# Retention layer and gated feed-forward on one core: the decay table by products instead of Exp rows, a moved table load, and one queue for the first loads

## The chip, the cores and the metric

The kernel runs on 1 core of a Trainium2 chip. The metric is device time in microseconds (us) of one execution. Each median below is over all runs. The kernel before was run again on the same chip beside every group of experiments, with medians of 248.31 to 248.34 us. A ratio is the mean time of one kernel's runs over that of the other's in the same rounds, so it is not quite the ratio of the medians that I quote.

PE is the matmul engine, ACT is ScalarE, DVE is VectorE, POOL is GpSimd, and SP is SyncE, which here only issues loads and stores. In this kernel PE's results stand in PSUM and all other tiles in SBUF; an eviction is the copy of a result from PSUM to SBUF. A load lands when its data are there.

"Span" is the length of the profiled execution in its trace; it is some 1.7 us shorter than that execution's time. "Granted clock" is the mean share of full speed that PE, the matmul engine, was given.

## The reference

Two stages. The first is a retention recurrence over q, k, v of shape (4 batches, 8 heads, 768 tokens, 64):

```python
gamma = 1.0 - 2.0 ** (-5.0 - np.arange(H, dtype=np.float32))
scale = 1.0 / np.sqrt(D)
for t in range(S):
    state = gamma[None, :, None, None] * state + np.einsum('bhd,bhe->bhde', k[:, :, t], v[:, :, t])
    y[:, :, t] = scale * np.einsum('bhd,bhde->bhe', q[:, :, t], state)
```

The second takes y, as 3072 tokens of 512, through a feed-forward layer with d_ff = 1536:

```python
gate = 1.0 / (1.0 + np.exp(-(x @ w_gate)))
val = x @ w_val
return (gate * val @ w_out).astype(np.float32)
```

## The kernel before

The recurrence is cut into chunks of 128 tokens, six to a batch. Decay is taken out of the recurrence: v is multiplied by a table `tabv` that grows with the token, and the sum is multiplied by a table `taby` that shrinks with it. `taby` holds scale x gamma^t for 768 tokens and all heads, two heads in the partitions of each of 4 blocks of columns. ScalarE (ACT) makes it, row by row:

```python
def make_taby(cols):
    for p in range(NP):          # NP = 4
        nc.scalar.activation(taby[:, p, cols], toky[:, cols], AX.Exp, scale=lgp[:, p:p + 1], bias=lsc)

def transposes(g):
    # ... 8 transposes of kn[g], qn[g] on PE into the one PSUM buffer tp
    nc.scalar.activation(qkT[g], tp, AX.Copy)          # the eviction

def scale_v(g, eng):                                   # both inputs in SBUF
    eng.tensor_tensor(vs[g], vf[g], tabv[:, g % NCH, :].unsqueeze(2).to_broadcast([C, H, D]), op=ALU.mult)

def y_out(g):                                          # y is in PSUM, taby in SBUF
    # ...
    nc.vector.tensor_tensor(xT[g // 4][:, :, col:col + C], y[g], taby[:, :, c * C:(c + 1) * C], op=ALU.mult)
```

The loads are issued in the order of use. Chunk 0 comes over the queues of SP and ScalarE as f32, everything else over GpSimd's (POOL) queue, which casts k, q and the weights to bf16 on the way (v stays f32):

```python
nc.sync.dma_start(out=kf, in_=src(k, 0))
nc.scalar.dma_start(out=qf, in_=src(q, 0))
load_v(0, nc.sync)
# ... iota for toky over 768 columns, load_chunk(1), load_chunk(2)
load_gate_val(0)
load_chunk(3)
for s in range(1, NFF // 2):
    load_gate_val(s)
load_chunk(4)
for s in range(4):
    load_out(s)
for g in range(5, 8):
    load_chunk(g)
```

The start of the kernel is scheduled by hand. `keep_on(n)` is n small products that are meant to keep PE's clock up while it waits:

```python
make_taby(slice(0, 256))
# ... casts of chunk 0
keep_on(36); transposes(0); keep_on(8); scale_v(0, nc.vector); scores(0); state(0); state_out(0); masks(0); keep_on(8)
make_taby(slice(256, 384))
transposes(1); scale_v(1, nc.vector); inter(0); intra(0); y_out(0)
keep_on(10); scores(1); state(1); state_out(1); masks(1); inter(1); keep_on(10)
make_taby(slice(384, 512))
transposes(2); intra(1); scale_v(2, nc.vector); y_out(1)
# ... chunk 2 likewise
make_taby(slice(512, 768))
nc.scalar.preload_act_table(AX.Sigmoid)
intra(2); y_out(2); scale_v(3, nc.vector); keep_on(8)
up(0, 0, 0, 384)                                       # the first up-projection
```

After that, attention of later chunks is woven into the feed-forward products, in a fixed order on PE.

Of the kernel before, what the change touches and what calls it, by code (L numbers as in the profile page):

```python
# [9 lines left out]
F32 = mybir.dt.float32  # L10
BF16 = mybir.dt.bfloat16
I32 = mybir.dt.int32
AX = mybir.ActivationFunctionType
ALU = mybir.AluOpType
# [3 lines left out]
def kernel(  # L18
# [10 lines left out]
    nc = tc.nc  # L29
    B, H, S, D = q.shape  # L30
# [4 lines left out]
    NP = H // 2  # L35
    KT = D_MODEL // 128
    NFF = D_FF // 128
    scale = 1.0 / math.sqrt(D)
    lg = [math.log(1.0 - 2.0 ** (-5.0 - h)) for h in range(H)]

    ctx.enter_context(tc.manual_schedule())
    const = ctx.enter_context(tc.tile_pool(name="const", bufs=1))
# [12 lines left out]
    def src(x, g):  # L55
        b, c = divmod(g, NCH)
        return x[b, :, c * C:(c + 1) * C, :].rearrange("h s d -> s h d")

    def load_v(g, eng):
        vf[g] = ld.tile([C, H, D], F32, tag="vf", name="vf", bufs=8)  # L60
        eng.dma_start(out=vf[g], in_=src(v, g))  # L61

    def load_kq(g):
        kn[g] = ld.tile([C, H, D], BF16, tag="kn", name="kn")
        qn[g] = ld.tile([C, H, D], BF16, tag="qn", name="qn")
        nc.gpsimd.dma_start(out=kn[g], in_=src(k, g))  # L66
        nc.gpsimd.dma_start(out=qn[g], in_=src(q, g))  # L67

    def load_chunk(g):
        load_kq(g)  # L70
        load_v(g, nc.gpsimd)
# [5 lines left out]
    def load_gate_val(s):  # L77
        cols = slice(s * 256, (s + 1) * 256)
        for dst, w in ((wg, moe_w_gate), (wv, moe_w_val)):
            nc.gpsimd.dma_start(out=dst[:, :, cols],  # L80
                                in_=w.rearrange("(kk p) n -> p kk n", p=128)[:, :, cols])
# [6 lines left out]
    kf = const.tile([C, H, D], F32, name="kf")  # L88
    qf = const.tile([C, H, D], F32, name="qf")
    nc.sync.dma_start(out=kf, in_=src(k, 0))  # L90
    nc.scalar.dma_start(out=qf, in_=src(q, 0))
    load_v(0, nc.sync)
    tokv = const.tile([128, NCH], I32, name="tokv")
    nc.gpsimd.iota(tokv, pattern=[[C, NCH]], base=0, channel_multiplier=1)
    ident = const.tile([128, 128], BF16, name="ident")
    make_identity(nc, ident)
    toky = const.tile([128, S], I32, name="toky")
    nc.gpsimd.iota(toky, pattern=[[1, S]], base=0, channel_multiplier=0)
    load_chunk(1)
    causal = const.tile([128, 128], F32, name="causal")  # L100
    nc.gpsimd.memset(causal, 1.0)
# [7 lines left out]
    lgp = const.tile([128, NP], F32, name="lgp")  # L109
    lsc = const.tile([128, 1], F32, name="lsc")  # L110
    nc.vector.memset(lsc, math.log(scale))
    for p in range(NP):
        nc.vector.memset(lgp[0:D, p:p + 1], lg[2 * p])
        nc.vector.memset(lgp[D:128, p:p + 1], lg[2 * p + 1])
    zbd = [const.tile([128, NP, C], BF16, name=f"zbd{i}") for i in range(2)]
    for t in zbd:
        nc.vector.memset(t, 0.0)
    taby = const.tile([128, NP, S], F32, name="taby")

    def make_taby(cols):  # L120
        for p in range(NP):
            nc.scalar.activation(taby[:, p, cols], toky[:, cols], AX.Exp, scale=lgp[:, p:p + 1], bias=lsc)  # L122

    causal4 = causal.unsqueeze(1).to_broadcast([128, NP, 128])

# [4 lines left out]
    def pair(t, p):  # L130
        return t[:, 2 * p:2 * p + 2, :].rearrange("s h d -> s (h d)")

    def transposes(g):
        tp = pa.tile([128, 2 * NP, C], BF16, tag="tp", name="tp")
        for i, x in enumerate((kn[g], qn[g])):
            for p in range(NP):
                nc.tensor.transpose(tp[:, i * NP + p, :], pair(x, p), ident)  # L137
        qkT[g] = at.tile([128, 2 * NP, C], BF16, tag="qkT", name="qkT", bufs=3)
        nc.scalar.activation(qkT[g], tp, AX.Copy)  # L139

    def scale_v(g, eng):
        vs[g] = ld.tile([C, H, D], BF16, tag="vs", name="vs", bufs=4)
        eng.tensor_tensor(vs[g], vf[g], tabv[:, g % NCH, :].unsqueeze(2).to_broadcast([C, H, D]),  # L143
                          op=ALU.mult)
# [16 lines left out]
    def inter(g):  # L161
        y[g] = pa.tile([128, NP, C], F32, tag="y", name="y")
        if g % NCH > 0:
            for p in range(NP):
                nc.tensor.matmul(y[g][:, p, :], zbd[(g - 1) % 2][:, p, :], qkT[g][:, NP + p, :],  # L165
                                 start=(p == 0), stop=False, skip_group_check=True)
# [18 lines left out]
    def intra(g):  # L185
        first = g % NCH == 0
        for p in range(NP):
            for i, st in enumerate((stA[g], stB[g])):
                nc.tensor.matmul(y[g][i * D:(i + 1) * D, p, :], vs[g][:, 2 * p + i, :], st[:, p, :],  # L189
                                 start=(first and p == 0), stop=True, skip_group_check=True)  # L190
# [60 lines left out]
    def keep_on(n):  # L251
        u = pf.tile([128, 512], F32, tag="ff", name="ff")
        for _ in range(n):
            nc.tensor.matmul(u[:, :128], ident, ident, start=True, stop=True)  # L254


    load_gate_val(0)
    load_chunk(3)
    for s in range(1, NFF // 2):
        load_gate_val(s)  # L260
    load_chunk(4)
    for s in range(4):
        load_out(s)
# [2 lines left out]

    kn[0] = ld.tile([C, H, D], BF16, tag="kn", name="kn")
    qn[0] = ld.tile([C, H, D], BF16, tag="qn", name="qn")
    make_taby(slice(0, 256))
    nc.vector.tensor_copy(kn[0], kf)  # L270
    nc.scalar.copy(qn[0], qf)
    keep_on(36)
# [5 lines left out]
    state_out(0)  # L278
    masks(0)
    keep_on(8)  # L280
    make_taby(slice(256, 384))
    transposes(1)
    scale_v(1, nc.vector)
    inter(0)
# [5 lines left out]
    state_out(1)  # L290
    masks(1)
    inter(1)
    keep_on(10)
    make_taby(slice(384, 512))
    transposes(2)
    intra(1)
    scale_v(2, nc.vector)
    y_out(1)
# [4 lines left out]
    masks(2)  # L303
    inter(2)
    keep_on(12)
    make_taby(slice(512, 768))
    nc.scalar.preload_act_table(AX.Sigmoid)  # L307
    intra(2)
    y_out(2)
    scale_v(3, nc.vector)  # L310
# [62 lines left out]
```

## Time and profile before

| kernel before | value |
|---|---|
| time | 248.33 us (three runs, 248.3 to 248.36) |
| span, granted clock of the profiled run | 246.4 us, 0.997 |
| first up-projection on PE | 18.98 us |
| q of chunk 5: landed, transposed | 43.68, 44.72 us |

The page's first part gives busy time of each engine, its share of the span, and the number of instructions:

```profile
PE 234.1 (95%) x1816; PEld 123.3 (50%) x1816; DVE 101.5 (41%) x168; ACT 106.0 (43%) x191; POOL 91.5 (37%) x111
```

PE is busy for 95% of the span, so it idles for some 12 us at most. Here is the timeline of VectorE (DVE) before, around the end of chunk 0. Its columns are start, length, engine, line, operation, output and inputs, shapes, and in brackets the idle time before it and what ended that:

```profile
9.63 0.69 DVE L143 TENSOR_TENSOR vs<-vf,tabv 128x512 bf16<-128x512 f32 x1 [0.30 <-DMA vf<-in_v_dram]
10.24 0.68 DVE L197 TENSOR_TENSOR xT<-y,taby 128x512 bf16<-128x512 f32 x1
```

Two multiplications of the same size, each some 0.7 us, one right behind the other.

### The profile page before, as it was taken

How to read it: one execution, taken by the hardware profiler on the slowest of the kernel's cores; microseconds unless marked ns; L12 is line 12 of the kernel's file. 1: busy time of each engine (PE TensorE's matmuls, PEld its weight loads, DVE VectorE, ACT ScalarE, POOL GpSimd, SP SyncE). 2: the span in 40 equal slices, each digit the busy share in tenths (PEclk: the TensorE clock that was granted, in tenths of full speed). 3: DMA queues.
4: the chain of work that ended last, by engine and by line, in shares of the span. 5: the costliest groups of instructions: out<-in, count | busy, mean ns of one | idle time of the engine just before them, and what ended most of it. 6: DMA issues, size and time to landing. Idle time of an engine off the chain costs nothing.

```text
span 246.4 us, 4449 instructions
## 1 busy us (share of the span) xinstructions
PE 234.1 (95%) x1816; PEld 123.3 (50%) x1816; DVE 101.5 (41%) x168; ACT 106.0 (43%) x191; POOL 91.5 (37%) x111
## 2 busy tenths in 40 slices
PE   7689998997999999999999999999999999999993
PEld 7565644554455554445554445544445554444441
DVE  2565444563446631246631256541256532234300
ACT  7788333425444431454443444342444542233221
POOL 8986574987999912961111001111000000000000
PEclk9999999999999999999999999999999999999998
DMA  9999999999999932994012100002100002200022
GB/s 146 181 198 196 192 213 203 176 208 232 229 174 127 188 80 84 145 180 61 3 41 78 54 3 3 0 17 92 64 0 3 0 0 88 85 0 3 0 85 85
DMA packets 64212, 24.13 MB, mean 98 GB/s; under 512 B 51969, under 2 KB 59649, under 8 KB 64193
## 3 DMA queue, kind: packets, MB, share of 16 engines
q0 software_dynamic: 57616, 16.78, 62.2%
q1 hardware_dynamic: 5536, 6.82, 8.2%
q10 hardware_dynamic: 1040, 0.26, 0.5%
q8 instruction: 14, 0.23, 0.4%
q14 instruction: 6, 0.04, 0.1%
HBM read 28.31 MB, written 6.29 MB: 140 GB/s over the span
## 4 chain that ended last, share of the span: by engine, by line
PE 91%; ACT 7%; issue 1%; DVE 0%; POOL 0%; POOLq 0%; ACTq 0%
PE ff L234 50%; PE ff L244 26%; PE tp L137 4%; PE sA L153 3%; ACT qkT L139 2%; PE y L189 2%; ACT taby L122 2%; PE z L175 2%; PE y L165 2%; PE ff L254 2%; ACT zbd L183 1%; ACT L307 1%; ACT ob L247 0%; ACT gs L238 0%; DVE xT L197 0%
## 5 line engine op out<-in xcount | busy, mean ns | idle before, releaser
L239 DVE TENSOR_TENSOR hT<-gs,ff 128x512 bf16<-128x512 f32 (+2 forms) x76 | 50.1, 660 | 85.6 <-PE ff L234 81.9
L234 PE MATMUL ff<-xT,wg 128*128 128x512 bf16 (+2 forms) x304 | 74.7, 368 | 1.2 <-DVE xT L197 1.1
L234 PE MATMUL ff<-xT,wv 128*128 128x512 bf16 (+2 forms) x304 | 74.6, 368 | 0.0
L238 ACT ACTIVATE gs<-ff 128x512 f32<-128x512 f32 (+2 forms) x76 | 43.6, 573 | 55.4 <-PE ff L234 55.4
L244 PE MATMUL ff<-wo,hT 128*128 128x512 bf16 x288 | 65.0, 379 | 0.0
L234 PEld LDWEIGHTS <-wv 128*128 128x128 bf16 x304 | 29.3, 98 | 33.2
L244 PEld LDWEIGHTS <-hT 128*128 128x128 bf16 x288 | 27.3, 98 | 32.1
L234 PEld LDWEIGHTS <-wg 128*128 128x128 bf16 x304 | 27.4, 98 | 28.4 <-issue 1.4
L143 POOL TENSOR_TENSOR vs<-vf,tabv 128x512 bf16<-128x512 f32 x16 | 16.6, 1058 | 65.0 <-PE y L189 60.1
L247 ACT COPY ob<-ff 128x512 f32<-128x512 f32 x24 | 14.1, 586 | 54.9 <-PE ff L244 50.5
L139 ACT ACTIVATE qkT<-tp 128x1024 bf16<-128x1024 bf16 x24 | 24.6, 1024 | 13.4 <-PE tp L137 13.3
L197 DVE TENSOR_TENSOR xT<-y,taby 128x512 bf16<-128x512 f32 x24 | 16.4, 684 | 20.6 <-PE y L189 20.6
L158 DVE TENSOR_TENSOR stA<-sA,causal 128x512 bf16<-128x512 f32 x24 | 16.5, 687 | 19.9 <-PE sB L153 19.9
L61 POOL DMA_DIRECT2D vf<-in_v_dram x23 | 21.0, 913 | 5.0 <-issue 2.0
L66 POOL DMA_DIRECT2D kn<-in_k_dram x23 | 21.0, 913 | 3.3 <-DMA wo<-in_moe_w_out_dram 1.7
L67 POOL DMA_DIRECT2D qn<-in_q_dram x23 | 20.6, 897 | 2.6 <-DMA wo<-in_moe_w_out_dram 1.7
L183 ACT CAST zbd<-z 64x256 bf16<-64x256 f32 x40 | 14.7, 367 | 12.1 <-PE z L175 11.8
L159 DVE TENSOR_TENSOR stB<-sB,causal 128x512 bf16<-128x512 f32 x24 | 16.3, 680 | 0.0
L153 PE MATMUL sA<-qkT 64*128 64x128 bf16 x96 | 9.5, 219 | 5.5 <-ACT qkT L139 5.4
L153 PEld LDWEIGHTS <-qkT 64*128 64x128 bf16 x192 | 5.4, 94 | 10.6 <-ACT qkT L139 6.8
L254 PE MATMUL ff<-ident 128*128 128x128 bf16 x104 | 9.0, 252 | 1.6 <-POOL ident masks.py:199 1.6
L189 PE MATMUL y<-stA,vs 128*64 128x128 bf16 x96 | 9.9, 222 | 0.0
(36 smaller groups left out, 123.1 us busy)
## 6 DMA issues: line engine op xcount, KB each, us to landing
out_dram<-ob SPq DMA_DIRECT2D x24, 256.0 KB, 2.0
vf<-in_v_dram POOLq DMA_DIRECT2D x23, 256.0 KB, 7.2
kn<-in_k_dram POOLq DMA_DIRECT2D x23, 128.0 KB, 7.2
qn<-in_q_dram POOLq DMA_DIRECT2D x23, 128.0 KB, 7.1
wg<-in_moe_w_gate_dram POOLq DMA_DIRECT2D x6, 256.0 KB, 8.7
wv<-in_moe_w_val_dram POOLq DMA_DIRECT2D x6, 256.0 KB, 9.2
wo<-in_moe_w_out_dram POOLq DMA_DIRECT2D x4, 384.0 KB, 10.7
qf<-in_q_dram ACTq DMA_DIRECT2D x1, 256.0 KB, 4.5
```

What stands on the lines that cost most here:

```text
L61: eng.dma_start(out=vf[g], in_=src(v, g))
L66: nc.gpsimd.dma_start(out=kn[g], in_=src(k, g))
L67: nc.gpsimd.dma_start(out=qn[g], in_=src(q, g))
L139: nc.scalar.activation(qkT[g], tp, AX.Copy)
L143: eng.tensor_tensor(vs[g], vf[g], tabv[:, g % NCH, :].unsqueeze(2).to_broadcast([C, H, D]), op=ALU.mult)
L153: nc.tensor.matmul(sc[g][i][:, p, :], t[half, p, :], t[half, NP + p, :], start=True, stop=True)
L158: nc.vector.tensor_tensor(stA[g], sc[g][0], causal4, op=ALU.mult)
L183: nc.scalar.copy(zbd[g % 2][half, :, half], zps[b][half])
L234: nc.tensor.matmul(u[:, lo:hi], w[:, kk, n1 * 128:(n1 + 1) * 128], xT[t][:, kk, lo:hi], start=(kk == 0), stop=(kk == KT - 1))
L238: nc.scalar.activation(gs[:, lo:hi], ps[0][:, lo:hi], AX.Sigmoid)
L239: nc.vector.tensor_tensor(hT[t][:, n1, lo:hi], gs[:, lo:hi], ps[1][:, lo:hi], op=ALU.mult)
L244: nc.tensor.matmul(o, hT[t][:, n1, sm * 128:(sm + 1) * 128], wo[:, n1, :], start=(n1 == 0), stop=(n1 == NFF - 1))
```

## The change

The intent: the Exp rows of `taby` stand in ScalarE's queue in front of evictions that PE waits for. gamma^(t+256) is gamma^t x gamma^256, so only 256 columns need Exp and the others are two products with a constant per head, given to GpSimd. The sigmoid table then loads earlier, behind an eviction, and ScalarE no longer issues a load.

```diff
-    nc.scalar.dma_start(out=qf, in_=src(q, 0))
+    nc.sync.dma_start(out=qf, in_=src(q, 0))
+    nc.scalar.preload_act_table(AX.Exp)
...
-    toky = const.tile([128, S], I32, name="toky")
-    nc.gpsimd.iota(toky, pattern=[[1, S]], base=0, channel_multiplier=0)
+    toky = const.tile([128, 256], I32, name="toky")
+    nc.gpsimd.iota(toky, pattern=[[1, 256]], base=0, channel_multiplier=0)
...
+    gup = {i: const.tile([128, NP], F32, name=f"gup{i}") for i in (1, 2)}
+    for i, t in gup.items():
+        for h in range(H):
+            nc.vector.memset(t[h % 2 * D:(h % 2 + 1) * D, h // 2:h // 2 + 1], math.exp(256 * i * lg[h]))
...
-    def make_taby(cols):
-        ...
+    for p in range(NP):
+        nc.scalar.activation(taby[:, p, 0:256], toky, AX.Exp, scale=lgp[:, p:p + 1], bias=lsc)
+
+    def extend_taby(i):
+        nc.gpsimd.tensor_tensor(taby[:, :, i * 256:(i + 1) * 256], taby[:, :, 0:256],
+                                gup[i].unsqueeze(2).to_broadcast([128, NP, 256]), op=ALU.mult)
...
     load_gate_val(0)
+    extend_taby(1)
     load_chunk(3)
     for s in range(1, NFF // 2):
         load_gate_val(s)
+    extend_taby(2)
     load_chunk(4)
...
-    make_taby(slice(0, 256))
...
-    make_taby(slice(256, 384))
     transposes(1)
...
-    keep_on(10)
-    make_taby(slice(384, 512))
+    keep_on(4)
     transposes(2)
+    nc.scalar.preload_act_table(AX.Sigmoid)
...
-    make_taby(slice(512, 768))
-    nc.scalar.preload_act_table(AX.Sigmoid)
```

More of the change, by code (lines that the diff above doesn't have):

```diff
@@ L118 @@
     taby = const.tile([128, NP, S], F32, name="taby")
-    def make_taby(cols):
-        for p in range(NP):
-            nc.scalar.activation(taby[:, p, cols], toky[:, cols], AX.Exp, scale=lgp[:, p:p + 1], bias=lsc)
+    for p in range(NP):
[3 more added lines that the diff above has]
+                                gup[i].unsqueeze(2).to_broadcast([128, NP, 256]), op=ALU.mult)
     causal4 = causal.unsqueeze(1).to_broadcast([128, NP, 128])
```

## The prediction

> **What bounds the kernel now.** I read the page first, then the chain of waits over the first 60 us, then the timelines of ScalarE, PE, VectorE and GpSimd there, and last the landing time of every load. On the page, the chain and the row of DMA shares by slice (40 slices of 6.16 us):
>
> ```profile
> DMA  9999999999999932994012100002100002200022
> ...
> PE 91%; ACT 7%; issue 1%; DVE 0%; POOL 0%; POOLq 0%; ACTq 0%
> ```
>
> PE holds 91% of the chain, so the body of the kernel is matmul work that this change leaves alone. Only the 7% of ScalarE can be shortened. The DMA row is the warning: the engines are 90% busy or more in the first 14 slices, up to 86 us, so any gain at the start brings PE closer to loads that do not come sooner. The timeline of ScalarE (start, length, what) shows where its share lies:
>
> ```profile
> 0.80 0.47 ACTq L91 DMA_DIRECT2D qf<-in_q_dram  x1
> 1.30 1.28 ACT L108 ACT_TABLE_LOAD   x1 [1.30 <-PEq L357]
> ...
> 9.01 1.65 ACT L122 ACTIVATE taby<-toky,lsc,lgp 128x128 f32<-128x128 int32 x4
> 10.68 1.02 ACT L139 ACTIVATE qkT<-tp 128x1024 bf16<-128x1024 bf16 x1
> ...
> 13.22 1.65 ACT L122 ACTIVATE taby<-toky,lsc,lgp 128x128 f32<-128x128 int32 x4
> 14.90 1.02 ACT L139 ACTIVATE qkT<-tp 128x1024 bf16<-128x1024 bf16 x1
> ...
> 17.47 2.07 ACT L122 ACTIVATE taby<-toky,lsc,lgp 128x256 f32<-128x256 int32 x4
> 19.57 1.28 ACT L307 ACT_TABLE_LOAD   x1
> 20.86 0.49 ACT L238 ACTIVATE gs<-ff 128x384 f32<-128x384 f32 x1
> 21.25 1.02 ACT L139 ACTIVATE qkT<-tp 128x1024 bf16<-128x1024 bf16 x1
> ```
>
> Up to 20 us each chunk is a ring: transposes on PE, their eviction qkT on ScalarE, scores on PE, masks on VectorE, products on PE, y times taby on VectorE. The evictions of chunks 1 and 2 each start the moment four table rows end, though their transposes were done at 9.2 and 13.7 us. The ring takes 4.22 us (10.68 to 14.90). PE's timeline shows three more places that I need, first up-projection and chunk 5's transposes:
>
> ```profile
> 18.98 0.81 PE L234 MATMUL ff<-xT,wg 128*128 128x384 bf16 x4 [0.30 <-DVE xT L197]
> ...
> 44.49 0.39 PE L137 MATMUL tp<-ident,kn 128*128 128x128 bf16 x4
> 44.72 0.39 PE L137 MATMUL tp<-ident,qn 128*128 128x128 bf16 x4
> ```
>
> From 18.98 on PE has almost no gaps: one of 1.12 us at 42.4 and one of 1.18 us at 57.1, both behind evictions, and both unchanged. So the gain is what the first up-projection moves forward, less any wait that appears later. For such waits I read the loads of chunk 5. Its q load is issued by GpSimd at 32.88 us; asked by tile, that one instruction gives:
>
> ```profile
> L67 POOL DMA_DIRECT2D qn<-in_q_dram x1: 873/873/873, 32.9 to 32.9; - x1
> ...
> DMA to landing us min/median/max: 10.8/10.8/10.8
> ```
>
> 32.88 + 10.80 = 43.68 us. PE transposes it at 44.72, so today it has 1.04 us to spare. This is the number that decides my prediction.
>
> **What the Trainium skill says.** "ScalarE: Activation LUTs", What ACT_TABLE_LOAD costs, gives about 1283 ns for a load plus a drain of about 1380 ns, and 280 + 0.833 N ns for an activation with a pointer bias, 93 more for a pointer scale. The trace agrees on the load (1283 ns, twice) and on the rows (586 ns worked out for 256 columns, 587 in the group; 480 against 482 for 128), but shows no drain: the sigmoid starts 0.01 us after the load ends. "GPSIMD Engine Reference", 3.1 Elementwise, has a product of two f32 tensors at 4497 ns for 2048 columns, so some 2.2 us for 1024; the trace has 1058 ns for 512 columns (vs on GpSimd), so 2.1 us, and I use that. "DMA: Bandwidth & Descriptors", Issuing engines are not separate DMA queues, says that issuing from several engines saves only issue time, as all DMAs run on the same 16 engines. Here the two queues did bring more: some 224 to 287 GB/s in the half microseconds from 2.5 to 4.5 us while both ran, about 219 at 4.5 to 5.0 with nearly one alone (bytes of the packets by the time they ended). So one queue can cost the last of the three loads something.
>
> **The change, part by part.**
>
> Removed from ScalarE: eight Exp rows of 128 columns (2 x 1.65 = 3.30 us) and four of 256 (2.07 us), 5.37 us in all. The sigmoid table load (1.28 us) is moved, not removed.
>
> Chunk 0. ScalarE gives its 0.47 us of issuing to SP, so the Exp table load starts at about 0.8 instead of 1.30 and the first rows end near 4.9 instead of 5.35. The q of chunk 0 landed at 5.33; behind k on one queue I expect 5.0 to 5.3, hence its cast ends at 5.6 to 5.9 instead of 5.96. The k cast does not help sooner, because PE is in its 36 warm-up products until about 5.4. Gain 0.0 to 0.3 us. The v of chunk 0 (6.60) may land 0.3 to 0.6 later, which its use at 7.86 nearly absorbs. VectorE gets 16 memsets at about 0.105 us apart, 1.7 us, in a stretch in which it waited 2.3 us for k: free.
>
> Chunk 1. The eviction no longer waits for rows; ScalarE is free at about 8.8 and the transposes are done at about 9.2. It starts near 9.3 instead of 10.68: 1.4 us.
>
> Chunk 2. Not another 1.65. After the eviction of chunk 1 the ring goes through VectorE: v of chunk 1 lands at 9.61, scaling it and y of chunk 0 end at about 10.95, PE needs that y buffer back for chunk 1 (11.0 to 11.3), then 4 warm-up products instead of 10, then transposes to about 12.2. Eviction near 12.3 instead of 14.90: 2.6 us in all. The v of chunk 2 lands at 12.52; scaling, y of chunk 1 and two masks, at 0.60 to 0.69 us each, end at about 15.2; products and y of chunk 2 end at 16.3. First up-projection at about 16.3 instead of 18.98: **2.6 to 2.7 us**.
>
> Chunk 3. The 2.07 + 1.28 us ahead of the sigmoid look like the largest item but bring almost nothing on top: PE had the second up-projection to do until 22.2 and the scores of chunk 3 began at 22.32. The table load now stands between an eviction and state copies, 0.75 us of idle time, and its other 0.5 delays only copies needed much later. The load of v for chunk 3 lands at 18.56, and VectorE will now wait some 2.2 us for it; in my schedule its two up-projection products and masks still end at 21.7, when PE wants them.
>
> GpSimd gets two products of about 2.1 us and a shorter iota (0.77 to about 0.33 us). The first delays the issue of chunk 3's loads by 1.6 us net. They were issued at 9.85 but landed at 16.63, behind a backlog, so the queue should just stay fed. The second, near 22 us, falls where up to eight loads are outstanding and the issues wait for landings anyway: hidden.
>
> Then the loss. PE arrives at chunk 5's transposes 2.7 us sooner, at 42.0 for q, but q lands at 43.68, or perhaps 0.2 sooner, as the GpSimd queue starts 0.4 us sooner but meets chunk 0's loads. PE works in order, so it stands for 1.5 to 1.7 us. Chunk 6's q (landed 46.69, used 48.88) has 2.2 us to spare and then suffices. Sum: 2.7 - 1.5 = **1.2 us**, 248.33 to 247.1 us.
>
> **The rivals.** (1) *The whole 2.7 us arrive*, about 245.7 us. For it: ScalarE is plainly the wait in the ring. Against it: the DMA row and the 1.04 us of slack; it needs the loads to land 1.6 us sooner, with the same bytes in the same order. (2) *The GpSimd products starve the DMA queue.* For it: issues of chunk 3 move 1.6 us later, and if the product takes 3 us beside VectorE the queue runs empty for up to a microsecond; all later loads then move, and the gain is 0.0 to 0.5 us, about 248.1 us. Against it: an issue-to-landing time of 6.8 us there, against 3.7 for one with an idle queue (73.43 to 77.14). (3) *The one queue for chunk 0 delays v or q* enough to eat the chunk 1 gain. Bounded by about 0.6 us at the start, and chunk 5's wait would swallow such a loss anyway, so the time stays 247.1.
>
> **Range and chances.** The limit is a landing time whose shift I put at -0.9 to +0.5 us, so the gain is 0.5 to 1.9 us: 246.4 to 247.8, and with 0.1 to 0.2 for the chip a range of 246.3 to 248.0. Two per cent is 5 us; all that leaves ScalarE's chain is 5.4 us plus the moved load and most of that was not on PE's path. So within 2% is nearly certain.
>
> **What would show it.** In the profile after: no wait of an eviction for table rows, qkT of chunks 1 and 2 near 9.3 and 12.3; first up-projection near 16.3 (if 17.5, the ring through VectorE and loads is tighter than I think); each GpSimd product 2.0 to 2.4 us; a new idle time of PE of about 1.5 us before chunk 5's transposes near 42 to 43.6, put down to a DMA of kn or qn; that landing within 0.5 us of 43.5. If no such gap is there and the time is near 245.7, rival 1 holds and I misjudged the loads. If loads from chunk 3 on land over 0.5 us later than before, rival 2 holds.

## The result, and the profile after

| | before | after |
|---|---|---|
| median | 248.31 us (4 runs, 248.23 to 248.36) | 248.08 us (4 runs, 247.61 to 248.28) |
| ratio, 95% interval | | 0.9988 (0.9971 to 1.0005) |
| span of the trace | 246.4 us | 245.9 us |

The times are the same within the interval. The gain of the medians is 0.23 us where 1.2 was predicted, and 248.08 lies just above the predicted range. The first question is where the other microsecond went. On the page of the changed kernel, the busy times, the DMA shares by slice, and the chain of waits:

```profile
PE 234.7 (95%) x1810; PEld 123.7 (50%) x1810; DVE 103.4 (42%) x184; ACT 100.8 (41%) x179; POOL 94.9 (39%) x113
...
DMA  8999999999999992994012100002100002200022
...
PE 79%; DMA 11%; POOL 6%; ACT 1%; issue 0%; DVE 0%; POOLq 0%; ACTq 0%
```

ScalarE did 5.2 us less work and its share of the chain fell from 7% to 1%. The share alone doesn't show that the part aimed at is gone: up to the landing of chunk 5's q the chain now runs through GpSimd (6%) and loads (DMA, 11%) and no longer through PE and ScalarE at the start. The timeline of ScalarE after shows it in place:

```profile
10.27 1.02 ACT L147 ACTIVATE qkT<-tp 128x1024 bf16<-128x1024 bf16 x1 [0.24 <-PE tp L145]
...
13.71 1.02 ACT L147 ACTIVATE qkT<-tp 128x1024 bf16<-128x1024 bf16 x1 [0.58 <-PE tp L145]
14.75 1.28 ACT L303 ACT_TABLE_LOAD   x1
```

Both evictions now wait for PE's transposes, and no longer for table rows. The table load sits behind the second one. But the evictions start at 10.27 and 13.71, where the prediction had 9.3 and 12.3: PE itself is late. VectorE's timeline shows why:

```profile
8.17 0.69 DVE L151 TENSOR_TENSOR vs<-vf,tabv 128x512 bf16<-128x512 f32 x1 [3.30 <-DMA vf<-in_v_dram]
...
10.20 1.77 DVE L151 TENSOR_TENSOR vs<-vf,tabv 128x512 bf16<-128x512 f32 x1
11.89 0.68 DVE L205 TENSOR_TENSOR xT<-y,taby 128x512 bf16<-128x512 f32 x1
```

Compare the second and third line with the two of before. The scaling of chunk 1's v takes 1.77 us instead of 0.69, and y of chunk 0 begins at 11.89 instead of 10.24. v had landed at 10.17, so this is no wait for data. GpSimd's timeline for the same stretch, by the same columns:

```profile
9.45 1.96 POOL L129 TENSOR_TENSOR taby<-taby,gup 128x1024 f32<-128x1024 f32 x1
11.29 0.95 POOL L66 DMA_DIRECT2D kn<-in_k_dram  x1
```

The new product runs from 9.45 to 11.41; the scaling starts inside it and ends at 11.97, 0.56 us (most of its usual 0.69) behind it. It looks as if VectorE had stood still until the product was over. Also, the first line of VectorE shows that v of chunk 0 landed late, at 8.07 us.

PE's timeline after, first up-projection and chunk 5's transposes:

```profile
17.91 0.81 PE L242 MATMUL ff<-xT,wg 128*128 128x384 bf16 x4 [0.30 <-DVE xT L205]
...
43.45 0.39 PE L145 MATMUL tp<-ident,kn 128*128 128x128 bf16 x4
44.16 0.40 PE L145 MATMUL tp<-ident,qn 128*128 128x128 bf16 x4 [0.33 <-DMA qn<-in_q_dram]
```

The first up-projection gained 18.98 - 17.91 = 1.07 us. The k transposes of chunk 5 gained 44.49 - 43.45 = 1.04 us, so all of it is still there. Then PE idles for 0.33 us for q, and behind it the gain is 44.72 - 44.16 = 0.56 us, which is what is left in the span (246.4 to 245.9). This profiled run was the fastest of the four (247.61 us); the two slowest, 248.26 and 248.28, had a granted clock of 0.99, so the trace shows less than the whole loss of the median. The load of q, asked for by tile in the trace after, was issued at 33.31 us:

```profile
L67 POOL DMA_DIRECT2D qn<-in_q_dram x1: 873/873/873, 33.3 to 33.3; - x1
...
DMA to landing us min/median/max: 10.8/10.8/10.8
```

33.31 + 10.80 = 44.12 us: it landed 0.44 us later than before, and PE went on 0.04 us after it. The transfer took as long as before (10.80 us); it was issued 0.43 us later.

### The profile page after: what moved, and what is told of

It reads as the page before. It is cut to its first block, busy times and chain, and to the rows that moved or that the text cites. A ratio compares the mean times of both kernels' runs of the same rounds, so it can differ in the third digit from the quotient of the medians. Undisturbed runs are those within 1.5% of the kernel's fastest.

```text
span 245.9 us, 4445 instructions
## 1 busy us (share of the span) xinstructions
PE 234.7 (95%) x1810; PEld 123.7 (50%) x1810; DVE 103.4 (42%) x184; ACT 100.8 (41%) x179; POOL 94.9 (39%) x113
## 4 chain that ended last, share of the span: by engine, by line
PE 79%; DMA 11%; POOL 6%; ACT 1%; issue 0%; DVE 0%; POOLq 0%; ACTq 0%
PE ff L242 43%; PE ff L252 26%; DMA wv<-in_moe_w_val_dram 7%; DMA qn<-in_q_dram 4%; PE tp L145 3%; PE sA L161 2%; PE y L197 2%; PE z L183 2%; PE y L173 2%; POOL kn L66 1%; POOL vf L61 1%; POOL qn L67 1%; POOL taby L129 1%; POOL wg L80 1%; ACT ob L255 0%
## 5 line engine op out<-in xcount | busy, mean ns | idle before, releaser
L191 ACT CAST zbd<-z 64x256 bf16<-64x256 f32 x40 | 14.6, 366 | 12.6 <-PE z L183 12.3
L167 DVE TENSOR_TENSOR stB<-sB,causal 128x512 bf16<-128x512 f32 x24 | 16.3, 679 | 0.0
L145 PE MATMUL tp<-ident,qn 128*128 128x128 bf16 x96 | 9.5, 223 | 0.3 <-DMA qn<-in_q_dram 0.3
```

The costliest lines, as they stand in the source:

```text
L145: nc.tensor.transpose(tp[:, i * NP + p, :], pair(x, p), ident)
```

## The experiments

Three theories of the missing microsecond stood against each other. *The product theory*: GpSimd's product holds up VectorE's scaling of v, because both read two inputs from SBUF. *The queue theory*: the one queue for chunk 0 makes v of chunk 0 late (8.07 us), and the ring is late for that. *The landing theory*: nothing in the ring matters much, since PE waits for q of chunk 5 whatever comes before. The expectations name theories by letters in places: A is the queue theory, D the product theory, and B, E and F are rivals that are described where they come up. The sentence after each says in words what held. All kernels give the right result but two, which are marked.

### One queue or two

*e1*: the changed kernel with q of chunk 0 again on ScalarE's queue.

```diff
-    nc.sync.dma_start(out=qf, in_=src(q, 0))
+    nc.scalar.dma_start(out=qf, in_=src(q, 0))
```

> The changed kernel with the q of chunk 0 back on ScalarE's queue. Theory A (the loads slid because chunk 0's three loads share one queue): v of chunk 0 lands near 6.6 to 6.9 us instead of 8.07, the first up-projection starts near 16.8 instead of 17.91, q of chunk 5 lands near 43.6 instead of 44.12, PE waits for it some 1.5 us, time about 0.5 us under the changed kernel's (247.5). Theory B (they slid because the GpSimd queue starts 0.43 us sooner after the shorter iota): v of chunk 0 still lands after 7.3, q of chunk 5 near 44.1, time near 248.1.

Measured: 247.78 us (247.52 to 247.88), ratio 0.9976 (0.9963 to 0.9988). v of chunk 0 landed at 6.62, 1.45 us sooner than in the trace of the changed kernel, and still the first up-projection came at 17.82, only 0.09 us sooner. VectorE's timeline of this kernel:

```profile
6.72 1.91 DVE L151 TENSOR_TENSOR vs<-vf,tabv 128x512 bf16<-128x512 f32 x1 [1.58 <-DMA vf<-in_v_dram]
...
9.74 2.13 DVE L151 TENSOR_TENSOR vs<-vf,tabv 128x512 bf16<-128x512 f32 x1
```

Now both scalings are long. An early v is of no use, because the scaling ends at 8.63 all the same. This speaks against the queue theory (and v was not late, as B would have had it), and it adds a riddle, as the product shows in GpSimd's timeline only from 9.37 us, after the first scaling had ended.

*e5*: the kernel before with q of chunk 0 on SP's queue, the opposite edit of the same line.

> The kernel before with only one edit: q of chunk 0 behind k on SP's queue. Theory A: v of chunk 0 lands near 7.5 to 8.1 instead of 6.60, so its scaling holds the state product and everything behind it by about 1 us, the GpSimd loads land some 0.5 us later, and the time rises to about 249.3. Theory B: v of chunk 0 lands before 7.3, the loads where they were, 248.3 to 248.5.

Measured: 248.21 us (248.02 to 248.62), ratio 0.9999. v of chunk 0 landed at 6.47, q of chunk 5 at 43.50, first up-projection at 18.86. One queue by itself costs nothing here; the queue theory's expectation missed. One caution: over all traces, v of chunk 0 landed late (7.20 to 8.20 us) in 4 of 8 with one queue and in none of 9 with two (6.47 to 6.84). So few traces settle little, and this stays open; in the changed kernel the product hides such a delay.

### Chunk 5's loads ahead of most of w_out

*e2*: the changed kernel with the loads of chunk 5 issued behind the first quarter of w_out. *e3*: e1 and e2 together. *e4*: the kernel before with the edit of e2.

```diff
-    for s in range(4):
+    load_out(0)
+    load_chunk(5)
+    for s in range(1, 4):
         load_out(s)
-    for g in range(5, 8):
+    for g in range(6, 8):
         load_chunk(g)
```

> The changed kernel with chunk 5's loads issued ahead of three of the four w_out loads. If chunk 5's q landing sets the end, PE no longer waits at its transposes, they run near 43.7 instead of 44.16, and the time falls by about 0.5 us to 247.6, the 1.07 us of the first up-projection arriving whole. If something else sets it (the granted clock, the rate of PE's own work), the time stays at 248.1.

> Both edits: two queues for chunk 0 and chunk 5's loads ahead of three w_out loads. Theory A: first up-projection near 16.8, no DMA wait at chunk 5, some 2.1 us under the kernel before: 246.2. Theory B: the same as with chunk 5 ahead alone, 247.6.

> Control: the kernel before with chunk 5's loads ahead of three w_out loads. Chunk 5's q had 1.04 us to spare there, so nothing should change: 248.2 to 248.4.

Measured: e2 247.22 us (247.21 to 247.76), ratio 0.9961 (0.9948 to 0.9973); e4 248.27 us (248.2 to 248.34), ratio 0.9998. In e2, q of chunk 5 landed at 37.93, and PE's timeline has no idle time before its transposes:

```profile
43.43 0.39 PE L145 MATMUL tp<-ident,kn 128*128 128x128 bf16 x4
43.66 0.39 PE L145 MATMUL tp<-ident,qn 128*128 128x128 bf16 x4
```

44.72 - 43.66 = 1.06 us: the whole gain of the ring passes, and the time falls by 248.31 - 247.22 = 1.09 us. The same edit does nothing for the kernel before, which never waited there. So the landing theory holds for the second part of the loss, and only for that: the ring itself gives 1.07, not 2.65.

e3 came to 247.26 us (247.17 to 247.78), as e2, and not to the 246.2 of the queue theory. Its profile fell in its slowest run, with a granted clock of 0.99, and is of little use for the ring.

### The product on VectorE

*e6*: the first product on VectorE, behind its cast of chunk 0's k, where it has idle time. *e7*: e6 with e1 and e2. *e12*: e6 with e2 alone.

```diff
-    def extend_taby(i):
-        nc.gpsimd.tensor_tensor(...)
+    def extend_taby(i, eng=nc.gpsimd):
+        eng.tensor_tensor(...)
...
     load_gate_val(0)
-    extend_taby(1)
...
     nc.vector.tensor_copy(kn[0], kf)
+    extend_taby(1, nc.vector)
```

> The changed kernel with the first table product on VectorE, in its idle time before v of chunk 0 lands, instead of on GpSimd. Theory D (while GpSimd runs the product, VectorE's multiplies with two SBUF inputs, the scalings of v for chunks 0 and 1, are held: 1.43 to 2.13 us instead of 0.69): both scalings take 0.69 us again, the first up-projection starts near 16.5 instead of 17.9, PE then waits about 1.5 us for q of chunk 5, and the time is about that of the two-queue run or a little better, 247.4 to 247.8, with no half-clock run. Rival E (the scalings are slowed by the DMA queue's descriptors or by the loads themselves): they stay at 1.4 to 2.1 us and the first up-projection stays at 17.8.

Measured: 249.43 us (248.4 to 249.88), ratio 1.004 (1.0021 to 1.0058): 0.4% slower than before, where I expected 247.4 to 247.8. Yet the ring did what the product theory says: both scalings took 0.693 us, and the first up-projection came at 16.83. The loss is at chunk 5. PE's timeline of e6:

```profile
43.86 0.40 PE L145 MATMUL tp<-ident,kn 128*128 128x128 bf16 x4 [1.55 <-DMA kn<-in_k_dram]
44.78 0.50 PE L145 MATMUL tp<-ident,qn 128*128 128x128 bf16 x3 [0.52 <-DMA qn<-in_q_dram]
```

PE arrived sooner and stood for 1.55 + 0.52 = 2.07 us. Half of that is because q itself landed 1.05 us later than before, at 44.73 (a likely reason comes with e12). And then its clock was halved. The view by stretches has, for each, its length, the busy times of PE, weight loads, VectorE, ScalarE and GpSimd, the granted clock, and DMA figures:

```profile
44.80:48.00 3.20, 3.20 (x11) 1.44 (x12) 0.69 (x1) 1.02 (x1) 2.91 (x4) 0.50 1.86 179
48.20:52.20 4.00, 3.95 (x48) 2.40 (x48) 2.23 (x4) 2.34 (x4) 3.61 (x5) 1.00 1.74 177
```

In 3.2 us only 11 matmuls were done at a clock of 0.50. From q of chunk 5 to q of chunk 6 PE took 5.79 us instead of 4.16, so this stretch behind the pause cost another 1.6 us. Sum: 2.15 us gained in the ring, 2.07 lost in waits, 1.63 lost to the clock, that is 1.55 slower; the span is 248.1 against 246.4. All six runs of e6 had a clock of 0.990 to 0.996. In e12 below, without the wait at chunk 5, the clock is 1.00 again. Making an early stage faster in front of a landing that does not come sooner can cost more than it saves.

> The same with two queues for chunk 0 and chunk 5's loads ahead of three w_out loads. Theory D with chunk 5's landing as the limit behind it: first up-projection near 16.3, 2.6 us sooner than the kernel before; chunk 5's q no longer awaited; chunk 6's q, which lands at 46.5 to 47.2 in the kernels with chunk 5 ahead, is now awaited by up to 1 us, so 1.7 to 2.6 us under the kernel before: 245.7 to 246.6. Rival E: 247.2, as without this edit.

Measured: **245.86 us** (4 runs, 245.79 to 246.03), ratio 0.9904 (0.9891 to 0.9917), the best and faster than both given kernels. VectorE's timeline and PE's:

```profile
5.51 1.22 DVE L129 TENSOR_TENSOR taby<-taby,gup 128x1024 f32<-128x1024 f32 x1 [0.32 <-ACT taby L126]
...
9.75 0.69 DVE L151 TENSOR_TENSOR vs<-vf,tabv 128x512 bf16<-128x512 f32 x1 [0.34 <-DMA vf<-in_v_dram]
```

```profile
42.04 0.39 PE L145 MATMUL tp<-ident,qn 128*128 128x128 bf16 x4
...
44.72 0.81 PE L252 MATMUL ff<-wo,hT 128*128 128x512 bf16 x3 [0.35 <-DMA wo<-in_moe_w_out_dram]
```

The product takes 1.22 us there, against 1.9 to 2.0 on GpSimd, and the scaling is back at 0.69. Evictions of chunks 1 and 2 start at 9.30 and 12.19 and the first up-projection at 16.34; the prediction had 9.3, 12.3 and 16.3. PE reaches chunk 5's q 2.68 us sooner than before without waiting. What is left is a wait of 0.35 us for the last part of w_out.

> The run with the product on VectorE took 249.4 us although its first up-projection came 2.15 us sooner than in the kernel before; its trace has PE waiting 2.1 us for chunk 5 and one half-clock window of 3.4 us behind that. Here chunk 5's loads go ahead of three w_out loads and nothing else changes. If that wait and the window are the whole loss: no wait for kn or qn of chunk 5, mean clock at 0.997 or above, time 246.0 to 246.5. If the product on VectorE costs something by itself, it stays above 247.

Measured: 246.75 us (246.42 to 247.0), ratio 0.9936 (0.9924 to 0.9948), a bit above what I expected. The ring is as in e7 (first up-projection 16.24), but PE waits 0.28 us for q of chunk 3 and 0.71 us for w_out. Two queues for chunk 0 thus go with 0.9 us here, through landings and not through the ring. The traces of e12 and e6 show a likely reason. Of e12, VectorE's timeline, then GpSimd's:

```profile
4.98 1.22 DVE L129 TENSOR_TENSOR taby<-taby,gup 128x1024 f32<-128x1024 f32 x1
```

```profile
5.09 1.27 POOL L103 TENSOR_SCALAR_AFFINE_SELECT causal<-causal 128x128 f32<-128x128 f32 x1
6.31 0.90 POOL L66 DMA_DIRECT2D kn<-in_k_dram  x1
```

And GpSimd's of e7, where the product, shown above, began at 5.51:

```profile
4.93 0.41 POOL L103 TENSOR_SCALAR_AFFINE_SELECT causal<-causal 128x128 f32<-128x128 f32 x1
5.29 0.90 POOL L66 DMA_DIRECT2D kn<-in_k_dram  x1
```

This looks like the same hold the other way round. VectorE's product began 0.11 us ahead of GpSimd's work on the causal mask, which reads SBUF, and that took 1.27 us, in e12 and e6 alone; in the other 15 traces it took 0.29 to 0.52. GpSimd's next load is then issued at 6.31 instead of 5.29. In e7 ScalarE issues one load first, so the table rows end later and the product begins behind the mask. No run takes apart how much of the late landings in e6 and e12 this 1.0 us explains.

### The product doubled, or added to the kernel before

*e8*: the first product done twice on GpSimd. *e9*: the kernel before with all its Exp rows, plus both products on GpSimd into a spare table that nobody reads.

> The changed kernel with the first table product done twice on GpSimd (the same values). Theory D: GpSimd's product lasts twice as long, so the two scalings of v together take about twice the added time (2 to 4 us more), first up-projection 19 to 21 instead of 17.9, time 249 to 250.5. Rival F (the product costs only by delaying the issue of the loads behind it): the scalings keep their lengths, chunk 3's loads are issued 1.9 us later and land up to 1 us later, time 248.3 to 249.

Measured: 252.86 us (250.58 to 253.15), ratio 1.0165. The scalings took 2.08 and 2.13 us, not twice the excess, and the first up-projection came at 17.99, so this part of the expectation missed: each scaling waits for one product only, it seems the one that is running. In the trace the time came from the loads. The pair took 4.25 us, chunk 3's loads were issued later, its v landed at 19.98 instead of 19.09, and q of chunk 5 landed at 47.00; PE waited 0.92 us at 23.8 and 1.31 + 0.56 at 46.1 and 47.0. The traced run is the fastest of the four (250.58 us, clock 1.00); the other three had clocks of 0.991 to 0.993 and took 2.0 to 2.6 us more, for which there is no trace.

> The kernel before with the two GpSimd products alone, written to a spare table that nobody reads; its own Exp rows stay. Theory D: scalings of v for chunks 0 and 1 end near 8.6 and 11 us, the state product of chunk 0 waits and everything behind it moves by some 0.8 us, time about 249.1. Rival E or F: scalings 0.69 us, time 248.3.

Measured: 249.2 us (249.0 to 249.82), ratio 1.0046 (1.0033 to 1.0059). The time was about as the product theory expected, but not by its mechanism. VectorE's timeline, then GpSimd's:

```profile
9.52 0.69 DVE L153 TENSOR_TENSOR vs<-vf,tabv 128x512 bf16<-128x512 f32 x1
```

```profile
9.90 2.05 POOL L131 TENSOR_TENSOR spare<-taby,gup 128x1024 f32<-128x1024 f32 x1
11.91 0.95 POOL L66 DMA_DIRECT2D kn<-in_k_dram  x1
```

Here the scaling was first: it began at 9.52, the product at 9.90, and the scaling kept its 0.69 us. The product took a little longer, 2.05 us instead of 1.96. So who starts first decides, as e12 shows more clearly. The 0.9 us were lost in loads: chunk 3's k was issued at 11.91, q of chunk 5 landed at 45.66, and PE waited 0.55 us for it, having used up its 1.04 us to spare. The first scaling, at 6.57, was not held here either, unlike in e1; why the early hold is missing, the runs do not show. In a kernel of another rhythm the prediction's second rival, products that delay the queue, is real.

### Where the early hold comes from

*e11*: e1, with the constants of the first product filled by VectorE only behind the scaling of chunk 0, so that no part of GpSimd can begin the product before.

```diff
+    fill_gup(2)
...
     scale_v(0, nc.vector)
+    fill_gup(1)
+    extend_taby(1)
     load_chunk(3)
```

> The two-queue variant of the changed kernel, with the factors of the first GpSimd product written by VectorE only after the scaling of v for chunk 0, so that no part of the product can start sooner. Theory D in its full form (part of GpSimd's cores start the product some 2.5 us before the profile shows it, because the loads queued ahead of it occupy other cores): the scaling of chunk 0 takes 0.69 us instead of 1.91, the one of chunk 1 stays at 1.4 to 2.1. If instead the scaling of chunk 0 was held by something other than the product, it stays at 1.9 us.

Measured: 247.73 us (247.66 to 248.58, the last at a clock of 0.99), ratio 0.9987. VectorE's timeline, then GpSimd's:

```profile
6.76 0.69 DVE L153 TENSOR_TENSOR vs<-vf,tabv 128x512 bf16<-128x512 f32 x1 [1.61 <-DMA vf<-in_v_dram]
...
9.70 2.19 DVE L153 TENSOR_TENSOR vs<-vf,tabv 128x512 bf16<-128x512 f32 x1 [0.22 <-DMA vf<-in_v_dram]
```

```profile
9.38 1.96 POOL L131 TENSOR_TENSOR taby<-taby,gup 128x1024 f32<-128x1024 f32 x1
```

The product stands at 9.38 for 1.96 us as in e1, but the first scaling fell from 1.91 to 0.69. So what held it in e1 was the product, free to begin early; most likely part of GpSimd was at work on it at 6.7 us, 2.6 us before the profile shows it. The first up-projection stayed at 17.84 (e1: 17.82): of the two scalings, chunk 1's alone binds.

### The changed kernel again, and without products

*e10*: the changed kernel, unchanged, in six more runs.

> The changed kernel itself once more, for its spread and a second trace. If its time hangs on when chunk 5's q lands and on whether a clock window falls to half after idle stretches of PE, the runs scatter over 0.5 us or more, those with a mean clock of 0.99 are the slow ones, and in the trace PE resumes within 0.1 us of that landing. If the first trace was an accident, the runs agree within 0.3 us.

Measured: 247.95 us (247.29 to 248.3), ratio 0.9982 (0.9969 to 0.9995). In its trace v of chunk 0 landed early, at 6.64, the scalings took 1.96 and 2.13 us, and the first up-projection came at 17.90, as with the late v. PE's timeline at chunk 5:

```profile
44.52 0.40 PE L145 MATMUL tp<-ident,qn 128*128 128x128 bf16 x4 [0.60 <-DMA qn<-in_q_dram]
```

q landed at 44.47 here and at 44.12 in the first trace; the gain left behind it is 44.72 - 44.52 = 0.20 us. The times of the ten runs of the changed kernel go from 247.29 to 248.30, with 247.29 and 248.3 both at a full clock. The scatter fits a landing that moves from run to run, while the kernel before, with a microsecond to spare there, stayed between 248.12 and 248.56 in all its runs. That is a fit, not a proof, as only two of those ten runs have a trace.

*e13* and *e14* (**wrong result**): the changed kernel without either product, y of every chunk taken with the first 256 columns; e14 with two queues for chunk 0 as well.

```diff
-        ... taby[:, :, c * C:(c + 1) * C], op=ALU.mult)
+        ... taby[:, :, c % 2 * C:(c % 2 + 1) * C], op=ALU.mult)
...
-    extend_taby(1)
...
-    extend_taby(2)
```

> The changed kernel with both GpSimd products left out; y of the later chunks takes the first 256 columns of the table, so the result is wrong on purpose. If the products are what makes the loads land later (44.12 and 44.47 for q of chunk 5 in two traces, 43.68 in the kernel before), it lands at 43.2 to 43.7 here; if the one queue of chunk 0 or the sooner start of GpSimd's queue does, it stays at 44.0 to 44.5. Scalings 0.69 us and first up-projection near 16.3 either way, PE waits 1.5 to 2.4 us at chunk 5, time 247.2 to 249.5 as that landing and the clock fall.

> The same (wrong result on purpose) with two queues for chunk 0. If neither products nor the queue are left to delay the loads, q of chunk 5 lands at 43.2 to 43.7, like the kernel before, PE waits there 1.5 to 1.8 us, and the time is 247.0 to 247.5, what my prediction had for the changed kernel. If it still lands at 44 or later, the sooner start of GpSimd's queue is the cause that is left.

Measured: e13 247.52 us (247.21 to 248.01), ratio 0.997; e14 247.5 us (247.38 to 247.61), ratio 0.9967. VectorE's scaling in e14, then PE's timeline:

```profile
9.87 0.69 DVE L151 TENSOR_TENSOR vs<-vf,tabv 128x512 bf16<-128x512 f32 x1 [0.36 <-DMA vf<-in_v_dram]
```

```profile
16.44 0.81 PE L242 MATMUL ff<-xT,wg 128*128 128x384 bf16 x4 [0.23 <-DVE xT L205]
...
43.05 0.40 PE L145 MATMUL tp<-ident,kn 128*128 128x128 bf16 x4 [1.01 <-DMA kn<-in_k_dram]
44.02 0.40 PE L145 MATMUL tp<-ident,qn 128*128 128x128 bf16 x4 [0.57 <-DMA qn<-in_q_dram]
```

Without products the ring is as predicted: 16.44 for 16.3. In e13, where v of chunk 0 landed at 8.20, it was 17.38, so with the product out of the way a late v does cost. And the landing of q of chunk 5, at 43.97 and 43.98, is still 0.3 us later than before. By these traces the products can account for 0.15 us (44.12) to 0.5 us (44.47) of the lateness in the changed kernel, if it isn't plain scatter. This also tells how to read the 6% of GpSimd in the chain after. The chain goes back from q through the queue to the product, but removing the product moved q by no more than that.

### One attempt at more

*e15*: e7 with the second product on VectorE too and v of chunk 5 behind w_out.

> Meant to beat both kernels: both products on VectorE, two queues for chunk 0, k and q of chunk 5 ahead of three w_out loads and its v behind them. The best run so far (245.86) still waited 0.35 us for the last w_out load at 44.72; this takes 1.0 us of loads from in front of it. First up-projection 16.3, no wait at chunk 5, none or under 0.2 us for w_out: 245.4 to 245.9.

Measured: 246.44 us (246.27 to 246.57), ratio 0.9922, worse than e7. The wait for w_out went away, but q of chunk 6 now landed at 46.91 and PE waited 0.46 us for it. The wait had moved: q of chunk 6 is transposed at 46.96, in e7 at 46.72, and the spans differ by about as much (244.5 and 244.2 us).

## Why the prediction was wrong, point by point

**What held.** ScalarE's rows left the path; every eviction of the start now waits for PE. No wait of PE was put down to the moved table load. What counts is the gain at the first up-projection less the waits that come later. The wait that came is the one that was named, q of chunk 5, with PE going on 0.04 us after the landing, and e2 shows that it was that one. The class, within 2%, was right.

**The first step that failed** is in "Chunk 2": "v of chunk 1 lands at 9.61, scaling it and y of chunk 0 end at about 10.95", and from it "First up-projection at about 16.3 instead of 18.98: 2.6 to 2.7 us". Measured: 17.91 and 17.90, a gain of 1.07. (Chunk 1's "near 9.3" failed too, with 10.27, but this did not bind: in e11 it was 9.26, and the first up-projection still came at 17.84.) The scaling took 1.77 to 2.13 us in the changed kernel's two traces, because GpSimd's product was running. The step priced the product as GpSimd's own time and as a delay of its queue. It allowed that the product might run slower beside VectorE (3 us, in the second rival), but never asked whether VectorE is held by it. The Trainium skill has the answer, on the page "SBUF — State Buffer", section Who interferes with whom: GpSimd's read port is one of VectorE's two, held like an exclusive lock, so a VectorE instruction with two inputs in SBUF contends with a GpSimd one that reads SBUF, and the order of issue decides which of them blocks. This case's traces agree in each part: the scaling with both inputs in SBUF went from 0.69 to as much as 2.19 us, y and the masks with one input in PSUM stayed at 0.67 to 0.69, and who was first was not held: the scaling in e9, VectorE's product in e12 and e6. The page was there to be read before predicting. That the first scaling was held before the product shows in the profile fits another section, "GPSIMD Engine Reference", 2.1 Instruction dispatch: its cores go on to the next instruction each as it finishes its own share, without waiting for one another. e11 shows that the product, begun early, is what holds it; that single cores ran ahead is then the likely reading, as the trace has one row for all of them.

The rest of that step was sound. With the product elsewhere (e7, e12) or absent (e14) the first up-projection came at 16.34, 16.24 and 16.44.

**The second step that failed** is in "Then the loss": "q lands at 43.68, or perhaps 0.2 sooner". It landed at 44.12 and 44.47, that is 0.44 and 0.79 us later, where the prediction allowed -0.9 to +0.5. So of 1.07 us gained, 0.51 and 0.87 were lost again, and 0.56 and 0.20 remained. This second step is the one by which the time was missed. By this sum the failed ring alone would have been hidden, and the right number would have been luck: had q landed at 43.68, PE could have kept nearly all of the 1.07, and the time would have been about 247.3, inside the range; e2, with no wait there, measured 247.22. Why it lands later is only partly known. One queue alone does not do it (e5, 43.50), products are not all of it (e13 and e14 without them, 43.97 and 43.98). The two traces of the changed kernel came to it by different ways. In the first the load was issued 0.43 us later and took 10.80 us as before, and q of chunk 1 was already half a microsecond late (8.9 us against 8.4), before the product starts in the profile. In the second q of chunk 1 was not late (8.2), chunk 5's load was issued 0.13 us later, and it took 11.46 us. So the two are not the same delay. Apart from e9, what the kernels with late landings have in common is the shorter iota and the earlier issue at the start (1.79 to 1.80 us instead of 2.22); this I have not taken apart, and it stays open.

**A smaller one.** Two of the changed kernel's ten runs had a granted clock of 0.99. Half-clock stretches behind idle time of PE were seen in e6 (1.6 us) and in e3's profiled run. The prediction had no term for a pause that costs more than its length.

**The rivals.** The first, all 2.7 us, is what e7 almost reaches. It needed what the prediction said it would, loads that land sooner, but also the product away from GpSimd: sooner loads alone gave 247.22 (e2) and 247.26 (e3). The second, a starved queue, is not the main cause in the changed kernel but is in e8 and e9. Its sign, loads over 0.5 us late from chunk 3 on, was met there only in part (k of chunk 3 17.34 for 16.63, its v 19.09 for 18.56, but q of chunk 5 by 0.44), and q of chunk 1, late before the product starts in the profile, speaks against it in the first trace. The third, one queue, costs nothing in e5, but e12 is 0.9 us behind e7. Its premise, that two queues bring more, does not hold either: in the trace after, the one queue alone moved 276 GB/s between 2.5 and 3.5 us.

## What to carry to other kernels

Before giving an elementwise product to GpSimd, look at which VectorE instructions run at that time with both inputs in SBUF; such a product may be cheaper in an idle gap of VectorE, here 1.22 us against 1.9. Its start matters there too: in e7 it held nothing, in e12, half a microsecond sooner, it held GpSimd for 1.0 us. When an early stage gets faster, find the next load that PE will meet and move it with the change, or the gain becomes a wait, and in e6 a half-speed stretch came on top of a wait of two microseconds. A wait at the bound may also make a kernel's times scatter, so its gain has to be judged over several runs and more than one trace.

## What the Trainium skill lacked or had wrong

- "SBUF — State Buffer", Who interferes with whom: right, and it explains the main surprise (0.69 to 2.19 us). The section itself lacks that the holder may not be visible yet ("Perfetto Trace Analysis", GPSIMD Engine Instruction, has the ground for it: the start in the profile is that of one of the eight cores). No page says how early, here some 2.6 us if that reading is right: in e1 the scaling was held from 6.72 to 8.63 us while the profile shows the product from 9.37 on; with the product kept back in e11 the scaling took 0.69.
- "ScalarE: Activation LUTs", What ACT_TABLE_LOAD costs: the drain of about 1380 ns on top of the load's 1283 was not seen. The next instruction started 0.01 to 0.02 us after the load in both given kernels, and the load 0.02 to 0.03 us after the one before it (after: load at 14.75 for 1.28, next at 16.05).
- "TensorE: Matmul & The Clock Gate", The HAM clock gate, What's actually happening, has a free-running window of 3413 ns, and the slow clock come after at least one idle window. The length agrees: the slow stretch in e6 lasted 3.41 us at 0.50. But PE's idle time just before it was 2.07 us in two pieces, less than a whole window.
- "GPSIMD Engine Reference", 3.1 Elementwise: the 2.2 us estimated from its figure (of an add of 2048 columns) for a product of 1024 were 1.91 to 2.05 us for single products in the traces, so it was a little high.
- "DMA: Bandwidth & Descriptors", Issuing engines are not separate DMA queues: e5 agrees (one queue, ratio 0.9999). No page gives the spread of one and the same load's landing from run to run, 44.12 and 44.47 us in two traces of the same kernel, which here decided the time.
